# Another order for the first 200 steps of a fused window attention and gated MLP kernel on one core

## The chip, the cores and the metric

The kernel runs on one core of a Trainium2 chip. The core has five engines with their own instruction queues, each worked through in order: TensorE (PE in the profile; its weight loads are PEld), VectorE (DVE), ScalarE (ACT), GpSimd (POOL) and SyncE (SP). An engine waits on semaphores that other engines and the DMA transfers raise. SP and POOL issue all DMAs here. SP's go into one DMA queue (q1), POOL's into another (q0); POOL's are those that turn float32 in HBM into bfloat16 on the way.

The metric is the device time of one execution in microseconds, the median of several. The profile is of one execution.

## What is computed

Four batches, 8 heads, 768 positions, head size 64. Causal attention with a window of 128 and 4 sink positions, and behind it a block with a gelu, a layer norm over one half, a product over the positions (w_sg), a gate and an output product with a residual:

```python
scores = scale * np.matmul(q, k.transpose(0, 1, 3, 2))
keep = is_sink | in_window
scores = np.where(keep, scores, -1000000000.0)
a = softmax(scores)
x = heads_side_by_side(np.matmul(a, v))
...
h = gelu(x @ w_in)
u, v = (h[..., :d_ff // 2], h[..., d_ff // 2:])
v_n = (v - mu) / np.sqrt(var + 1e-06) * g_ln
v_s = np.einsum('ts,bsd->btd', w_sg, v_n) + b_sg[None, :, None]
return x + (u * v_s) @ w_out
```

## The kernel before

The kernel is one list of steps, `STEPS`, written out by hand. A step is a name and indices (`QK.0.1.2`: batch 0, head pair 1, group 2), and a last letter often gives the engine (A ScalarE, D VectorE, P GpSimd). A loop calls the function of each step in the order of the list; each engine then works through its own instructions in that order, with semaphores where data or buffers demand it. Nothing reorders them. So the list sets the order within each engine and within each DMA queue, and no more than that: a step of one engine may stand far ahead of another's and run later.

The stages of a batch, with the functions and their lines in the kernel before:

- **Loading q and k.** Batch 0 comes in as eight pairs of heads in float32 through SP (`LPQ`, `LPK`, L245, 384 KB each), is cast to bfloat16 by some engine (`CPQ`, `CPK`; `cast` and `copy`, L197 to L204), transposed on TensorE (`TQ`, `TK`, L376) and copied out of PSUM (`EQ`, `EK`, L199 and L200). Batches 1 to 3 come in as bfloat16 through POOL, in tiles of 128 positions with all heads (`LQ.b.i`, `LK.b.i`, L225, 128 KB written each). A transpose step of batch 1 or 2 (`TQ.b.g`, `TK.b.g`, L382) takes tiles 2g and 2g+1. Batch 3 is transposed by DMA (`DQ`, `DK`).
- **v and the weights.** `LVH.b.i` (L271) loads v of four heads through POOL, two per batch. `LW.0` and `LW.1` (L277) load the halves of w_in for v and for u, `LWS` (L282) the halves of w_sg, `LWO` (L285) w_out, `LB` (L301) b_sg. `LC` (L289) brings v's sink rows and `LG` (L292) the rows of g_ln through SP; `GTR` and `GCP` turn g_ln. POOL has eight semaphores for its loads, used in turn, so a load waits until the one eight before it has landed.
- **Attention.** `QK` (L483) makes the scores of two heads in one of two PSUM buffers (`sc`), `EX` (L488) the exponentials on ScalarE into one of ten `P` buffers. The window is cut out by `MK`: a product with a mask on VectorE (L495), or two selects on GpSimd (L498, L501). A `QK` step with a last index of 1 first multiplies the identity with a large negative bias (L478), and then needs no mask. `KS`, `SK` and `SX` do the sinks, `VSM` scales v's sink rows. `AV` (L524 to L531) multiplies with v into one of four PSUM buffers (`mm`), `NR` (L540, L541) divides by the sum. `XT` and `XE` transpose the result.
- **The block behind it.** `MV` and `GV` (L566, L570) make the v half of h and its gelu, `BN`, `RS`, `NM` and `Z` (L579 to L600) the layer norm, where `RS` runs on GpSimd. `MU` and `GU` (L607, L612) make the u half. `WT` and `WE` (L619) transpose w_sg. `SP` (L627) is the product over positions, `GT` and `GM` (L632, L637) the gate, `OU` (L644) the output product, `RA` the residual and `ST` the store.
- **Helpers.** `HM.n` puts n matmuls on zeros ahead of the next PSUM buffer's use (L190). `TBL` touches the exponential or gelu function, so that ScalarE loads its table there. `WARM`, `FILL`, `MASK`, `MASK0`, `VSK`, `VSO`, `ZERO`, `IDEN` and `IDEN2` set up constants.

The stages of neighbouring batches are interleaved: the steps of batch 0's gate run among batch 1's attention, and so on. Of batch 2's tiles, `LK.2.0` and `LK.2.1` feed `TK.2.0`, whose place on TensorE is between `SP.0.0.3` and `QK.1.2.1`.

The scores and the mask, as the code has them:

```python
def QK(b, p, g, biased=0):
    sc = fresh(sc_ring, (b, p, g))
    w = wide(g)
    if biased:
        for hl in range(2):
            nc.tensor.matmul(sc[:, hl, 0:w], iden, (bias1 if g else bias0)[:, 0:w], start=True, stop=False)
```

Of the kernel before, what the change touches and what calls it, by code (L numbers as in the profile page):

```python
# [25 lines left out]
MK.0.1.0.D SX.0.1 SX.0.2 QK.0.3.1 MK.0.2.1.P GCP.D NR.0.0.0 EX.0.3.0 AV.0.0.1 AV.0.1.0 AV.0.1.1 NR.0.0.1 EX.0.3.1
QK.0.1.2 NR.0.1.0 AV.0.2.0 AV.0.3.0 EX.0.1.2 MK.0.3.1.P NR.0.1.1 QK.0.2.2 AV.0.2.1 NR.0.2.0 EX.0.2.2 TQ.1.0 NR.0.3.0
MK.0.1.2.P QK.0.3.2 AV.0.3.1 EQ.1.0.A NR.0.2.1 XT.0.0 NR.0.3.1 LWS.0 AV.0.0.2 EX.0.3.2 TBL.G AV.0.1.2 XE.0.0.D LK.1.1
XT.0.1 MK.0.2.2.D MV.0.0 XE.0.1.A LK.1.2 NR.0.0.2 MK.0.3.2.D LK.1.3 NR.0.1.2 AV.0.2.2 AV.0.3.2 LQ.1.2 NR.0.2.2 GV.0.0
MV.0.1 NR.0.3.2 LQ.1.3 BN.0.0 LWS.1 XT.0.2 GV.0.1 MU.0.1 XE.0.2.A BN.0.1 WT.0 GU.0.1 TK.1.0 MV.0.2 RS.0.1 EK.1.0.A  # L30
LK.1.4 NM.0.1 WE.0.A WT.1 GV.0.2 LK.1.5 TK.1.1 MU.0.2 LB.P EK.1.1.A BN.0.2 Z.0.0.A LK.2.0 WT.2 GU.0.2 MU.0.0 WE.1.D
RS.0.2 WE.2.D Z.0.1.A LQ.2.0 NM.0.2 Z.0.2.A Z.0.3.D Z.0.4.D WT.3 LQ.2.1 WT.4 GU.0.0 TBL.E WE.3.D WT.5 LQ.1.4 Z.0.5.D
TQ.1.1 QK.1.0.0 EQ.1.1.D QK.1.1.0 LQ.1.5 SP.0.0.0 WE.4.D LK.2.1 EX.1.0.0 VSM.1 SP.0.0.1 WE.5.D EX.1.1.0 LVH.1.0
GT.0.0.0 TK.1.2 KS.1 GT.0.0.1 QK.1.2.0 QK.1.3.0 EX.1.2.0 SP.0.0.2 LVH.1.1 GM.0.0.0.D EX.1.3.0 MK.1.2.0.D TQ.2.0
EK.1.2.A LQ.2.2 QK.1.0.1 EQ.2.0.D QK.1.1.1 TQ.1.2 EX.1.0.1 GT.0.0.2 LWO SP.0.0.3 EQ.1.2.D EX.1.1.1 LK.2.2 MK.1.0.1.D
# [41 lines left out]
def kernel(  # L77
# [412 lines left out]
    def MK(b, p, g, e="D"):  # L490
        w = wide(g)
        pt = P[b, p, g]
        if e == "D":
# [7 lines left out]
        nc.gpsimd.affine_select(out=p4[:, :, :, 128:256], in_=p4[:, :, :, 128:256],  # L501
                                compare_op=ALU.is_ge, fill=0.0, base=-1,
                                pattern=[[0, 2], [0, 2], [-1, 128]], channel_multiplier=1)
# [212 lines left out]
```

## Time and profile before

| what | value |
|---|---|
| median of 3 runs | 155.82 us (155.35 to 155.89) |
| profiled execution | 155.89 us |
| its span in the trace | 154.2 us |
| instructions | 3867 |
| TensorE busy | 145.7 us (95%) |
| VectorE busy | 122.9 us (80%) |
| ScalarE busy | 100.0 us (65%) |
| GpSimd busy | 99.7 us (65%) |
| granted TensorE clock | 1.00 |
| POOL's DMA queue q0 | 11.01 MB in 64608 packets |
| SP's DMA queue q1 | 13.41 MB in 22552 packets |
| SP.0.0.0 starts (first L627) | 38.91 us |

Times in the profile are microseconds from the start of the span. A matmul's busy time includes the fill and drain of the array, and successive matmuls overlap, so a busy TensorE need not run at its peak rate. The views used below: the timeline of one engine (start, duration, engine and line, operation, tile written and tiles read, shapes, how many merged, and in brackets the idle time ahead of it with what ended it), the chain of waits (the work that ended last, followed back from the end), the waits by engine, and the DMA issues of a stretch of time with their time from issue to landing.

### The profile page before, as it was taken

What the parts mean: (1) busy time and instruction counts of PE and PEld (TensorE: products, weight loads), DVE (VectorE), ACT (ScalarE), POOL (GpSimd) and SP (SyncE); (2) the same over time, 40 slices, a digit from 0 to 9 for tenths busy, and PEclk for the clock granted to TensorE, in tenths of its full rate; (3) what the DMA queues carried; (4) which work ended last, traced back from release to release, by engine and by line L of the source; (5) the groups of instructions that cost most, each with busy time, mean ns of one, the idle gap of its engine ahead of it and who ended that gap; (6) DMA issues with size and microseconds to landing.
All of it is one profiled execution on the core that took longest, in us unless ns stands there. A gap on an engine that the chain in (4) does not pass through costs nothing.

```text
span 154.2 us, 3867 instructions
## 1 busy us (share of the span) xinstructions
PE 145.7 (95%) x1540; PEld 94.5 (61%) x1554; DVE 122.9 (80%) x296; ACT 100.0 (65%) x117; POOL 99.7 (65%) x127
## 2 busy tenths in 40 slices
PE   6899899999999988999899999999999999999990
PEld 2355586879675765758466764486567644775550
DVE  4666889739989977797799887899789957867992
ACT  3699998799899766456987865369957122491000
POOL 4099799298999699999469769640798610400400
PEclk9999999999999999999999999999999999999999
DMA  4999999999999999999999399996510582410055
GB/s 158 305 351 157 154 195 204 166 189 211 148 141 154 185 155 140 147 150 156 156 223 250 81 276 177 185 190 81 211 72 1 105 221 73 150 54 20 0 203 206
DMA packets 87178, 24.67 MB, mean 160 GB/s; under 512 B 78772, under 2 KB 84920, under 8 KB 87160
## 3 DMA queue, kind: packets, MB, share of 16 engines
q0 software_dynamic: 64608, 11.01, 95.7%
q1 hardware_dynamic: 22552, 13.41, 33.0%
q8 instruction: 12, 0.20, 0.5%
q14 instruction: 6, 0.05, 0.1%
HBM read 24.81 MB, written 6.29 MB: 202 GB/s over the span
## 4 chain that ended last, share of the span: by engine, by line
PE 54%; POOL 18%; DMA 15%; ACT 4%; DVE 4%; issue 2%; SPq 1%; DVEq 0%; ACTq 0%; POOLq 0%
PE mm L627 15%; DMA v_sb<-in_v_dram 11%; PE mm L644 10%; PE sc L566 9%; PE sc L607 8%; POOL q L225 5%; POOL k L225 4%; DMA uT<-in_k_dram 4%; PE sc L483 4%; PE mm L524 3%; POOL v_sb L271 3%; PE mm L528 2%; POOL wsg_gated L637 2%; POOL P L498 2%; POOL P L501 2%
## 5 line engine op out<-in xcount | busy, mean ns | idle before, releaser
L488 ACT ACTIVATE P<-sc 128x1024 bf16<-128x1024 f32 (+1 forms) x48 | 43.4, 952 | 10.3 <-PE sc L483 10.1
L627 PE MATMUL mm<-wsgT,z 128*128 128x384 bf16 x192 | 34.4, 327 | 0.3 <-ACT z L597 0.3
L627 PEld LDWEIGHTS <-z 128*128 128x128 bf16 x192 | 17.6, 98 | 12.5 <-issue 0.7
L570 ACT ACTIVATE vt<-sc 128x1024 f32<-128x1024 f32 x12 | 12.3, 1027 | 18.4 <-PE sc L566 18.4
L632 DVE SCALAR_TENSOR_TENSOR gtmp<-mm,g_sb,b_bc 128x384 bf16<-128x384 f32 x32 | 19.0, 610 | 4.2 <-PE mm L627 4.0
L637 POOL TENSOR_TENSOR wsg_gated<-gtmp,uT 128x384 bf16<-128x384 bf16 x15 | 14.9, 1006 | 11.3 <-DVE gtmp L632 11.2
L607 PE MATMUL sc<-xT,w_in_sb 128*128 128x256 bf16 x192 | 22.1, 273 | 0.0
L566 PE MATMUL sc<-w_in_sb,xT 128*128 128x512 bf16 x92 | 21.8, 379 | 0.2
L644 PE MATMUL mm<-w_out_sb,wsg_gated 128*128 128x512 bf16 x85 | 21.2, 379 | 0.5
L498 POOL TENSOR_SCALAR_AFFINE_SELECT P<-P 128x512 bf16<-128x512 bf16 x21 | 13.7, 653 | 11.4 <-ACT P L488 11.4
L607 PEld LDWEIGHTS <-w_in_sb 128*128 128x128 bf16 x192 | 18.7, 98 | 2.9
L579 DVE BATCH_NORM_STATS2 st<-vt 128x6 f32<-128x512 f32 x24 | 15.4, 685 | 6.1 <-ACT vt L570 6.0
L541 DVE TENSOR_TENSOR x_sb<-mm,rcp 128x384 bf16<-128x384 f32 (+1 forms) x36 | 18.5, 513 | 1.2
L588 POOL TENSOR_TENSOR rs<-rs,neg_half 128x4 f32<-128x4 f32 (+1 forms) x8 | 7.1, 882 | 15.8 <-DVE rs L583 14.4
L225 POOL DMA_DIRECT2D k<-in_k_dram x18 | 16.4, 924 | 1.3 <-DMA v_sb<-in_v_dram 1.3
L648 DVE TENSOR_TENSOR ot<-mm,x_sb 128x512 f32<-128x512 f32 x23 | 15.4, 683 | 2.2 <-PE mm L644 2.2
L225 POOL DMA_DIRECT2D q<-in_q_dram x18 | 16.8, 956 | 0.0
L524 PE MATMUL mm<-v_sb,P 128*128 128x65 bf16 x192 | 16.1, 194 | 0.6 <-DVE x_sb L541 0.4
L524 PEld LDWEIGHTS <-P 128*128 128x128 bf16 x192 | 14.5, 97 | 2.5 <-DMA v_sb<-in_v_dram 0.6
L528 PE MATMUL mm<-v_sb,P 128*128 128x65 bf16 x160 | 15.4, 193 | 0.4 <-POOL P L501 0.4
L612 ACT ACTIVATE uT<-sc 128x1024 bf16<-128x1024 f32 x12 | 12.2, 1024 | 5.1 <-PE sc L607 5.1
L566 PEld LDWEIGHTS <-xT 128*128 128x128 bf16 x96 | 9.2, 98 | 10.1
(92 smaller groups left out, 242.9 us busy)
## 6 DMA issues: line engine op xcount, KB each, us to landing
out_dram<-ot SPq DMA_DIRECT2D x17, 256.0 KB, 2.5
v_sb<-in_v_dram POOLq DMA_DIRECT2D x8, 384.0 KB, 8.0
q<-in_q_dram POOLq DMA_DIRECT2D x18, 128.0 KB, 6.5
k<-in_k_dram POOLq DMA_DIRECT2D x18, 128.0 KB, 7.3
out_dram<-ot SPq DMA_DIRECT2D x14, 128.0 KB, 1.8
wsg_gated<-in_moe_w_sg_dram POOLq DMA_DIRECT2D x2, 576.0 KB, 8.4
w_in_sb<-in_moe_w_in_dram POOLq DMA_DIRECT2D x2, 512.0 KB, 9.0
uT<-in_q_dram SPq DMA_DIRECT2D x2, 384.0 KB, 3.0
```

The lines of the kernel that those rows point to most:

```text
L225: return nc.gpsimd.dma_start(out=dst.rearrange("p (h d) -> p h d", h=H), in_=heads(src, b, i))
L488: nc.scalar.activation(out=P.new((b, p, g))[:, :, 0:w], in_=sc_ring[b, p, g][:, :, 0:w], func=AF.Exp, scale=scale)
L498: nc.gpsimd.affine_select(out=p4[:, :, :, 0:128], in_=p4[:, :, :, 0:128], compare_op=ALU.is_ge, fill=0.0, base=0, pattern=[[0, 2], [0, 2], ...
L524: nc.tensor.matmul(av[:, il, hl, :], pt[:, hl, c:c + 128], vb[:, h, i, :], start=first, stop=False)
L528: nc.tensor.matmul(av[:, il, hl, :], pt[:, hl, c:c + 128], vb[:, h, i - 1, :], start=False, stop=(i < 2 and il == n - 1 and hl == 1))
L541: nc.vector.tensor_mul(x_sb.get(b)[:, i0:i0 + n, 128 * p:128 * (p + 1)].rearrange("p t (h d) -> p t h d", h=2), av[:, :, :, 0:Dh], rcp[:, ...
L566: nc.tensor.matmul(hp[:, jl, :], xT[b][:, 2 * g + jl, c, :], w_in_sb[:, c, d_half:2 * d_half], start=(c == 0), stop=(c == KD - 1))
L607: nc.tensor.matmul(hp[:, dc // 2, 256 * (dc % 2):256 * (dc % 2 + 1)], w_in_sb[:, c, 128 * dc:128 * (dc + 1)], xT[b][:, 2 * g:2 * g + 2, c, :],
L627: nc.tensor.matmul(ps[:, 0:NH], z[b][:, si, 128 * dc:128 * (dc + 1)], wsgT[:, si, NH * hf:NH * (hf + 1)], start=(si == 0), stop=(si == NT ...
L632: nc.vector.scalar_tensor_tensor(out=gtmp.new((b, hf, dc)), in0=mm_ring["g", b, hf, dc][:, 0:NH], scalar=g_sb[:, dc:dc + 1], in1=b_bc[:, N ...
L637: (nc.vector if e == "D" else nc.gpsimd).tensor_mul(gated(b, hf)[:, dc, :], gtmp[b, hf, dc], uT[b][:, dc, NH * hf:NH * (hf + 1)])
L644: nc.tensor.matmul(ps, gated(b, hf)[:, dc, 128 * tl:128 * (tl + 1)], w_out_sb[:, dc, :], start=(dc == 0), stop=(dc == KU - 1))
```

## The change

The first 200 or so steps are the same work in another order, up to `QK.1.3.0 EX.1.2.0`; from `SP.0.0.2` on the list is the same. The last letters and some forms differ:

- SP's loads are K0 Q0 G Q1 Q2 K1 K2 K3 Q3 (pairs of q and k, and `LG`) in place of Q0 K0 K1 Q1 Q2 G K2 K3 Q3.
- The casts of k pairs 0 and 1 and 2 are on VectorE (before: ScalarE, GpSimd, ScalarE), that of q pair 1 is on GpSimd (before: VectorE). GpSimd's `LVH.0.0` and `LVH.0.1` follow the cast of q pair 1 in place of that of k pair 1.
- `EQ.0.0` and `EQ.0.1` are on ScalarE, `EQ.0.2` on VectorE; before it was the other way round. `XE.0.0` is on ScalarE, `XE.0.1` and `XE.0.2` on VectorE.
- `QK.0.0.0` and `QK.0.1.0` are made with the bias, `QK.0.1.1` without it. The step `MK` with the letter N does nothing and marks such a group. `MK.0.1.1` and `MK.0.2.2` are on GpSimd; `MK.0.2.1` and `MK.0.1.2` on VectorE.
- `HM` counts are 9, 1, 1, 1, 2, 1, 2, 1 in place of 9, 4, 1, 3, 1, 3. Four of the new ones stand behind `AV.0.0.0`.
- The two `SK` steps stand behind `AV.0.1.0`, before they stood ahead of `AV.0.0.0`.
- `TQ.1.1` stands where `TQ.1.0` stood, and `TQ.1.0` later.
- The gelu table is loaded directly ahead of `GV.0.0`, the exponential's directly ahead of `EX.1.1.0`.
- POOL's loads behind `LVH.0.1`, as its queue has them:

```
before  LQ.1.0 LQ.1.1 LW.0 LK.1.0 LW.1 LWS.0 LK.1.1 LK.1.2 LK.1.3 LQ.1.2 LQ.1.3 LWS.1 LK.1.4 LK.1.5 LB LK.2.0 LQ.2.0 LQ.2.1 LQ.1.4 LQ.1.5 LK.2.1 LVH.1.0 LVH.1.1 LQ.2.2 LWO
after   LQ.1.3 LQ.1.2 LW.0 LWS.0 LW.1 LQ.1.1 LK.1.2 LQ.1.0 LK.1.1 LK.1.0 LWS.1 LQ.2.0 LK.1.4 LK.1.3 LK.1.5 LB LQ.1.4 LQ.2.1 LQ.1.5 LVH.1.0 LK.2.0 LK.2.1 LVH.1.1 LQ.2.2 LWO
```

- `RS.0.1` stands on GpSimd behind `LB` and ahead of `LQ.1.4`, `RS.0.2` between `LQ.1.5` and `LVH.1.0`; before, `RS.0.1` stood ahead of `LK.1.4` and `RS.0.2` ahead of `LQ.2.0`.

The diff, with the step list cut to the lines that are new:

```diff
-WARM LPQ.0 FILL LPK.0 LPK.1 LPQ.1 LPQ.2 LG MASK LPK.2 LPK.3 CPQ.0.A VSK LPQ.3 IDEN CPK.0.A IDEN2 MASK0 HM.9 TQ.0.0
-TK.0.0 EQ.0.0.D EK.0.0.A VSO HM.4 QK.0.0.0 ZERO CPK.1.P QK.0.0.1.1 EX.0.0.0 LVH.0.0 EX.0.0.1 QK.0.0.2.1 CPQ.1.D TK.0.1
...
+WARM LPK.0 LPQ.0 LG LPQ.1 CPQ.0.A IDEN FILL LPQ.2 CPK.0.D IDEN2 MASK ZERO HM.9 TK.0.0 EK.0.0.A HM.1 TQ.0.0 MASK0 VSK
+GTR VSO EQ.0.0.A HM.1 QK.0.0.0.1 EX.0.0.0 QK.0.0.1.1 CPQ.1.P LPK.1 TQ.0.1 QK.0.0.2.1 MK.0.0.0.N CPQ.2.D LPK.2 GCP.D
+EQ.0.1.A CPK.1.D EX.0.0.1 TK.0.1 LVH.0.0 TQ.0.2 CPK.2.D EQ.0.2.D LPK.3 LVH.0.1 TK.0.2 EK.0.1.A QK.0.1.0.1 CPK.3.P
+LQ.1.3 EX.0.0.2 LPQ.3 QK.0.1.1 EX.0.1.0 EX.0.1.1 LQ.1.2 TK.0.3 CPQ.3.D EK.0.2.D EK.0.3.A LW.0 TQ.0.3 HM.1 QK.0.2.1
+EX.0.2.1 QK.0.2.0 HM.2 AV.0.0.0 LC MK.0.0.1.N MK.0.1.0.N VSM.0 HM.1 AV.0.1.0 EQ.0.3.D KS.0 EX.0.2.0 SK.0.1 QK.0.3.1
+NR.0.0.0 SX.0.1 SK.0.2 NR.0.1.0 EX.0.3.1 MK.0.1.1.P AV.0.0.1 MK.0.2.0.D QK.0.3.0.1 AV.0.2.0 LWS.0 MK.0.2.1.D QK.0.1.2
+LW.1 SX.0.2 LQ.1.1 AV.0.1.1 NR.0.0.1 EX.0.3.0 NR.0.2.0 QK.0.2.2 MK.0.3.0.N AV.0.3.0 AV.0.2.1 MK.0.0.2.N EX.0.1.2
+MK.0.3.1.P NR.0.1.1 AV.0.3.1 QK.0.3.2 NR.0.3.0 NR.0.2.1 XT.0.0 LK.1.2 EX.0.2.2 XE.0.0.A NR.0.3.1 MK.0.2.2.P HM.2
+TQ.1.1 LQ.1.0 LK.1.1 XT.0.1 LK.1.0 AV.0.2.2 EX.0.3.2 LWS.1 AV.0.0.2 EQ.1.1.A MV.0.0 VSM.1 MK.0.1.2.D LQ.2.0 AV.0.1.2
+LK.1.4 XE.0.1.D MK.0.3.2.D GV.0.0 NR.0.0.2 NR.0.2.2 AV.0.3.2 LK.1.3 LK.1.5 NR.0.3.2 MV.0.1 NR.0.1.2 TBL.G.1 GV.0.1
+BN.0.0 XT.0.2 LB.P XE.0.2.D WT.1 BN.0.1 MU.0.1 MV.0.2 RS.0.1 WE.1.A WT.2 LQ.1.4 NM.0.1 TK.1.0 GU.0.1 MU.0.2 GV.0.2
+WE.2.D BN.0.2 HM.1 TQ.1.0 WT.3 Z.0.3.A MU.0.0 EK.1.0.A KS.1 LQ.2.1 Z.0.0.A EQ.1.0.D LQ.1.5 RS.0.2 GU.0.2 WT.0 LVH.1.0
+WT.4 TK.1.1 Z.0.2.A NM.0.2 Z.0.1.D Z.0.4.D LK.2.0 WE.3.A WE.0.D WT.5 WE.4.D Z.0.5.D GU.0.0 QK.1.1.0 LK.2.1 QK.1.0.0
+SP.0.0.1 WE.5.D EK.1.1.D SP.0.0.0 EX.1.1.0 TK.1.2 GT.0.0.1 QK.1.2.0 TBL.E.1 GT.0.0.0 EX.1.0.0 QK.1.3.0 EX.1.2.0
 SP.0.0.2 LVH.1.1 GM.0.0.0.D EX.1.3.0 MK.1.2.0.D TQ.2.0
...
-    def TBL(func):
+    def TBL(func, turn):
...
     def MK(b, p, g, e="D"):
         w = wide(g)
         pt = P[b, p, g]
+        if e == "N":
+            return
...
-        ps = mm_ring["o", b, t] if h else fresh(mm_ring, ("o", b, t))
+        ps = mm_ring["o", b, t] if ("o", b, t) in mm_ring.held else fresh(mm_ring, ("o", b, t))
```

More of the change, by code (lines that the diff above doesn't have):

```diff
@@ L26 @@
[L26 to L35, printed above, removed]
@@ new lines @@
+WT.4 TK.1.1 Z.0.2.A NM.0.2 Z.0.1.D Z.0.4.D LK.2.0 WE.3.A WE.0.D WT.5 WE.4.D Z.0.5.D GU.0.0 QK.1.1.0 LK.2.1 QK.1.0.0
+SP.0.0.1 WE.5.D EK.1.1.D SP.0.0.0 EX.1.1.0 TK.1.2 GT.0.0.1 QK.1.2.0 TBL.E.1 GT.0.0.0 EX.1.0.0 QK.1.3.0 EX.1.2.0
+SP.0.0.2 LVH.1.1 GM.0.0.0.D EX.1.3.0 MK.1.2.0.D TQ.2.0 EK.1.2.A LQ.2.2 QK.1.0.1 EQ.2.0.D QK.1.1.1 TQ.1.2 EX.1.0.1
+GT.0.0.2 LWO SP.0.0.3 EQ.1.2.D EX.1.1.1 LK.2.2 MK.1.0.1.D TK.2.0 MK.1.0.0.D QK.1.2.1 LK.2.3 EK.2.0.A QK.1.3.1
+MK.1.3.0.D SK.1.0 GM.0.0.1.D LQ.2.3 SP.0.1.0 EX.1.2.1 GT.0.0.3 MK.1.1.0.D LQ.2.4 EX.1.3.1 SP.0.1.1 MK.1.1.1.D LQ.2.5
@@ new lines @@
+MK.2.3.0.D TQ.2.1 LVH.2.0 TQ.2.2 EQ.2.1.D MV.1.0 EQ.2.2.D LQ.3.0 EK.2.2.D LQ.3.1 VSM.2 MU.1.0 GV.1.0 MK.2.1.0.D
+LVH.2.1 BN.1.0 MV.1.1 GU.1.0 LQ.3.2 RA.0.2 LQ.3.3 MK.2.0.0.D MV.1.2 GV.1.1 MK.2.2.0.D LK.3.1 KS.2 LK.3.2 BN.1.1 MU.1.1
+GV.1.2 LK.3.3 BN.1.2 RS.1.1 MU.1.2 GU.1.1 LQ.3.4 NM.1.1 Z.1.0.A RS.1.2 OU.0.3 GU.1.2 TBL.E.2 LQ.3.5 NM.1.2 Z.1.1.D
+SK.2.0 Z.1.4.D QK.2.0.1 Z.1.2.D Z.1.3.A QK.2.1.1 Z.1.5.D OU.0.4 RA.0.3 DK.3.0 SP.1.0.0 RA.0.4 SX.2.0 EX.2.0.1 SP.1.0.1
+GT.1.0.0 DQ.3.0 EX.2.1.1 GM.1.0.0.D SP.1.1.0 MK.2.0.1.P GT.1.0.1 QK.2.2.1 ST.0.3 GT.1.1.0 QK.2.3.1 GM.1.0.1.P DQ.3.1
```

63 lines of the change are left out of this document (27 added, 36 removed).

## The prediction

> **What bounds the kernel now.** I read, in order: the chain of waits (what the end hangs on), the timeline of each engine, and the DMA issues of short windows (issue to landing of one transfer). The profiled execution took 155.89 us: span 154.2 and 1.7 around it; the median of the runs is 155.82, so 0.07 less.
>
> The chain, us from start, length, what:
>
> ```profile
> 1.81 5.80 DMA uT<-in_k_dram
> ...
> 7.69 0.79 POOL k L204
> 8.48 8.04 DMA v_sb<-in_v_dram
> ...
> 42.11 9.21 DMA v_sb<-in_v_dram
> 51.36 0.50 issue
> 51.85 1.82 POOL k L225 x2
> ...
> 71.34 1.06 POOL rs L588
> ```
>
> Up to 16.5 us the end hangs on a load: the third pair lands at 7.61, POOL casts it, and only then issues v (LVH), which lands 8 us later. The chain comes back to POOL's loads from 36 to 52 us.
>
> TensorE, where it had to wait (timeline: start, us, operation, idle before and who ended it):
>
> ```profile
> 45.36 0.61 PE L382 MATMUL mm<-iden,k 128*128 128x128 bf16 x8
> ...
> 54.20 1.04 PE L644 MATMUL mm<-w_out_sb,wsg_gated 128*128 128x512 bf16 x3
> ...
> 55.83 0.40 PE L382 MATMUL mm<-iden,k 128*128 128x128 bf16 x4 [0.37 <-DMA k<-in_k_dram]
> ...
> 58.51 0.20 PE L528 MATMUL mm<-v_sb,P 128*128 128x65 bf16 x1 [0.39 <-POOL P L501]
> ```
>
> The first of these lines is step TK.2.0. Otherwise TensorE is full: busy 23.38 us of 16 to 40, 73.19 of 77 to 154. So a step's shift reaches the end unless one of these waits takes it up.
>
> Issues of a short window (KB, us from issue to landing):
>
> ```profile
> v_sb<-in_v_dram POOLq DMA_DIRECT2D x1, 384.0 KB, 7.2
> k<-in_k_dram POOLq DMA_DIRECT2D x1, 128.0 KB, 4.8
> ```
>
> These are LVH.1.0 and LK.2.1, and POOL issued them so:
>
> ```profile
> 39.85 0.91 POOL L225 DMA_DIRECT2D k<-in_k_dram  x1
> 40.71 2.86 POOL L271 DMA_DIRECT2D v_sb<-in_v_dram  x2
> ```
>
> So LK.2.1 landed at 39.85 + 4.8 = 44.6, LVH.1.0 at 40.71 + 7.2 = 47.9, LVH.1.1 at 42.11 + 9.2 = 51.3. Read one by one, POOL's loads land strictly in their order of issue, without a break, from LVH.0.0 (16.5) to LWO (54.2): a k or q tile lands 0.85 us after the one before it, a half of v 2.9 to 3.4, a half of w_in 2.5 to 2.6, of w_sg 2.8. This queue is full; a load's landing is its place in it.
>
> **The change part by part.**
>
> *Start of the queue.* LPQ.1 takes LPK.1's place as third pair, with the 2 KB of LG before it. Pairs landed at 3.85, 5.0, 7.6, 8.7, 9.7 (ends of the waits of their casts), two issues ahead of the data, so I take LG at nothing: third pair 7.6, POOL cast 0.8, LVH issued at 8.5, v at 16.5, all as before. GTR now needs g_rows before QK.0.0.0, at 6.4. Its landing there isn't shown: between 5.0 (pair ahead) and 7.6 (pair behind), 0 to 1.2; I take 0, and up to 16.5 the wait for v covers it.
>
> *ScalarE and VectorE until v.* ScalarE loses the casts of k pairs 0 and 2 (2 x 0.83) and gains EQ.0.0 and EQ.0.1, losing EQ.0.2 (+0.8): 0.86 less. VectorE gains three k casts (0.56 each), loses a q cast, the copies of EQ.0.0 and EQ.0.1 (0.95 each) and one 0.54 mask, and gains EQ.0.2. Followed pair by pair, k pair 1 is now fifth (9.7) and EK.0.1 ends near 11.5, against 11.3 before; EX.0.2.0 and .1, the seventh and eighth exponentials, end near 16.8, against 16.9. Nothing on the path. One more biased product of 384 columns (two matmuls, 0.33) lies there too.
>
> *TensorE after v.* The first AV starts at 16.56 as before. Behind it now stand HM.1, HM.2 and HM.1 (4 warm matmuls; a warm 128x512 starts every 0.216 us: 0.86) and the two SK groups that ran at 16.03 while TensorE waited (0.40): 1.26 more. Before had one wait in this part, 0.39 at 19.44, that these fill in part. The gelu table load (1.28) moves to directly ahead of GV.0.0, where MV.0.0 (1.7) runs over it; without that cover it would cost 1.28. WT, MU and MV change places among themselves; each load they need is due 0.5 us or more before it is used (LWS.0 and LW.1 follow LW.0, which landed at 22.9: 22.9 + 2.8 + 2.5 = 28.2, used at 29.3; LK.1.0 is five tiles later, 28.2 + 5 x 0.85 = 32.4, used at 33.3). So SP.0.0.1 starts 0.8 to 1.3 later; I take 1.1, near 40.0.
>
> *Loads of POOL.* This decides. Before, the end of this stretch was LK.2.0, LQ.2.0, LQ.2.1, LQ.1.4, LQ.1.5, LK.2.1, LVH.1.0, LVH.1.1. Now it is LVH.1.0, LK.2.0, LK.2.1, LVH.1.1. Ahead of LVH.1.1 stand the same 24 loads in both kernels; the 24th was LVH.1.0 and is now LK.2.1. It inherits that landing: 47.9 in place of 44.6. POOL's own waits don't break the queue: a load waits for the landing of the one eight before it, so LVH.1.0 is issued at about 37 and LK.2.1 by 40.2, in time; RS.0.1, behind LB, waits until 31.6 (before: 30.67), which the shift above holds.
>
> TK.2.0 reads LK.2.1. TensorE came to it at 45.36, now at 46.5 with the 1.1; it must stand until 47.95. All behind it (QK.1.2.1, QK.1.3.1, SK.1.0, SP.0.1.0) is late by 47.95 - 45.36 = 2.6, and the 1.1 is inside that. On ScalarE EK.2.0 and EX.1.2.1 wait with it, on VectorE MK.1.2.1.
>
> *What takes it up.* OU.0.0 waited for w_out until 54.2, TK.2.1 for k until 55.83, AV.1.3.1 for a POOL mask until 58.51. Places and landings of these loads are unchanged, POOL's masks too (its chain starts at 51.85, after LVH.1.1). Idle time there is 0.16 (the QK ahead ends at 54.04) + 0.37 + 0.39 = 0.92; start to start against the usual step it is 0.2 + 0.5 + 0.5 = 1.2, which I take. Left: 1.4. At 76.67 SP waits for z:
>
> ```profile
> 76.67 1.64 PE L627 MATMUL mm<-wsgT,z 128*128 128x384 bf16 x9 [0.26 <-ACT z L597]
> ```
>
> That z stood behind RS.1.1, which POOL began at 71.3 though its input was ready at 70.6; 1.4 later it begins at 72.0, so 0.35 more is taken up. Left 1.05. Behind that the order is unchanged and TensorE full, so it reaches the end.
>
> Sum: 155.89 + 2.6 - 1.2 - 0.35 = 156.94; beside the median, **156.9 us**.
>
> A clock row: the first nine warm matmuls ran in 3.71 us (0.42 each), later ones start every 0.216, and the granted clock is 1.00 in every window. The change has 14 warm matmuls ahead of the first AV where 21 stood (9 of them at the start in both); between 9.8 and 11.7 TensorE has only transposes.
>
> By the Trainium skill (TensorE: Matmul & The Clock Gate, Parts 1 and 4) an idle window of about 3.4 us brings the half clock back, and transposes don't count as busy in the same way; this gap would be under 2.5 us, so by that rule the sum stays.
>
> **The rivals.**
>
> - *Nothing takes up the 2.6.* VectorE is 4.00 busy of 4.00 at 44 to 48 and 48 to 52; held back by MK.1.2.1 it might be the next bound. Against: it waits 0.73 at 56.8 for TensorE, and most of its work there doesn't hang on TK.2.0. 155.9 + 2.6 = 158.5.
> - *Not slower: the queue starts earlier.* The third pair took 2.6 us behind the second, all others 1.0 to 1.2. If that was k's own bad luck, q pair 1 lands at 6.2; POOL's queue and all landings come 1.4 earlier. LK.2.1 lands at 46.5, TK.2.0 is 1.2 late, the three waits take that up, and a little of the wait for z too: 155.5. It decides from a landing of q pair 1 below 6.5 (1.05 gained); with 2 us gained (v at 14.5) it would be 154.9. For it: the odd 2.6. Against: it may belong to the third place.
> - *The queue doesn't pass the delay on* (LK.2.1 by 46.5, though behind LVH.1.0). Then 1.1 is left, which the 1.2 takes up: 155.8. Against: every landing read is in order.
> - *The half clock returns* for some 3.4 us ahead of the first AV: 1.7 of TensorE's time there, of which the wait for v hides half. TensorE would still be early enough for TK.2.0 at 47.95, so little is added: 157.3.
>
> **How the numbers follow.** Forecast 0.47; nothing taken up 0.14; earlier queue 0.25 (0.15 of it below 155.04); order not passed on 0.09; clock 0.05. The forecast's own range is 156.4 to 157.5 (uptake 0.9 to 1.3 and 0 to 0.4, landing +-0.4). Both signs hold chance, so the range goes from 155.0 (most of the earlier queue) to 158.6 (nothing taken up). About 0.5%, 0.78 us, is what a measurement can tell from no change: above 156.60 lie nearly four fifths of the forecast, the second and the last rival, 0.55; below 155.04 0.15; between 0.30.
>
> **What would show it.** Right: LVH.0.0 issued near 8.5 and the first AV near 16.5; LK.2.1 landing near 47.9; TensorE idle 1 to 2 us ahead of TK.2.0 with k's load as releaser; no wait left at 54.2, 55.8 and 58.5; z's wait near 77.7. Wrong: TK.2.0 without a wait, LVH.0.0 issued before 7.5, or SP.0.0.1 over 2 us later than 38.9.

## The result and the profile after

The changed kernel took 157.19 us (median of 4 runs, 157.07 to 157.55), the kernel before 155.58 us beside it (154.69 to 155.89): ratio 1.0117, 95% interval 1.0069 to 1.0164. A repeat of 12 runs on another occasion gave 1.0076 (1.0052 to 1.0101). So the change costs about 1%, 1.2 to 1.8 us. All ratios leave out runs more than 1.5% above the fastest of the same kernel. The profiled execution took 157.07 us, span 155.4, granted clock 1.00. The forecast of 156.9 us was near. Its mechanism was not the one that ran.

The chain of waits of the changed kernel (us from start, length, what), the answer to the first lines shown of before:

```profile
2.25 4.40 DMA uT<-in_q_dram
6.74 0.83 POOL q L205
7.57 1.84 POOL v_sb L272
9.41 9.13 DMA v_sb<-in_v_dram
...
46.55 2.25 DVE P L498 x3
48.80 0.98 DVE wsg_gated L640
49.79 0.54 DVE gtmp L635
50.37 1.14 PE mm L630 x6
```

The third pair, now q, landed at 6.65 (2.25 + 4.40), not at 7.6, so v was issued at 7.57 and not at 8.48. POOL's loads have left the chain around 42 to 52 us; three groups of VectorE (DVE) stand there instead.

TensorE of the changed kernel (timeline: start, us, operation, idle before and what ended it):

```profile
40.98 1.31 PE L630 MATMUL mm<-wsgT,z 128*128 128x384 bf16 x7 [0.34 <-DVE z L603]
...
46.61 0.61 PE L383 MATMUL mm<-iden,k 128*128 128x128 bf16 x8
...
50.37 0.81 PE L630 MATMUL mm<-wsgT,z 128*128 128x384 bf16 x4 [1.18 <-DVE gtmp L635]
...
56.58 1.04 PE L647 MATMUL mm<-w_out_sb,wsg_gated 128*128 128x512 bf16 x3
57.45 0.61 PE L383 MATMUL mm<-iden,k 128*128 128x128 bf16 x8
...
77.93 0.82 PE L630 MATMUL mm<-wsgT,z 128*128 128x384 bf16 x4 [0.37 <-ACT z L600]
```

TK.2.0 (46.61) has no bracket: it waited for nothing. LK.2.1 had landed at 46.4, read from its semaphore. The long wait is at 50.37, SP.0.1.1, which needs a PSUM buffer that GT.0.0.3 empties on VectorE. From 56 to 58 us the waits of before are gone: TensorE is later, and w_out and k were there earlier (w_out at 52.30 for 54.15 before, the later k tile of TK.2.1 at 53.97 for 55.78).

VectorE just ahead of that (same columns), in the changed kernel:

```profile
45.35 0.61 DVE L635 SCALAR_TENSOR_TENSOR gtmp<-mm,g_sb,b_bc 128x384 bf16<-128x384 f32 x1
45.87 0.68 DVE L201 COPY qT<-mm 128x1024 bf16<-128x1024 bf16 x1
46.47 2.33 DVE L498 TENSOR_TENSOR P<-P,mask 128x1024 bf16<-128x1024 bf16 x3
48.73 1.06 DVE L640 TENSOR_TENSOR wsg_gated<-gtmp,uT 128x384 bf16<-128x384 bf16 x1
49.71 0.60 DVE L635 SCALAR_TENSOR_TENSOR gtmp<-mm,g_sb,b_bc 128x384 bf16<-128x384 f32 x1
```

and POOL beside it:

```profile
45.81 2.64 POOL L226 DMA_DIRECT2D q<-in_q_dram  x3 [0.34 <-DMA v_sb<-in_v_dram]
48.44 1.13 POOL L640 TENSOR_TENSOR wsg_gated<-gtmp,uT 128x384 bf16<-128x384 bf16 x1
```

In the kernel before, POOL reached the same product a microsecond later:

```profile
46.88 2.72 POOL L225 DMA_DIRECT2D q<-in_q_dram  x3
49.50 1.03 POOL L637 TENSOR_TENSOR wsg_gated<-gtmp,uT 128x384 bf16<-128x384 bf16 x1
```

VectorE's lines are GT.0.0.2, EQ.1.2, three masks, GM.0.0.1, GT.0.0.3. The three masks took 2.33 us and GM.0.0.1 1.06; in the kernel before the same took 1.62 and 0.35:

```profile
44.09 0.61 DVE L632 SCALAR_TENSOR_TENSOR gtmp<-mm,g_sb,b_bc 128x384 bf16<-128x384 f32 x1
...
45.22 1.62 DVE L495 TENSOR_TENSOR P<-P,mask 128x1024 bf16<-128x1024 bf16 x3
46.75 0.35 DVE L637 TENSOR_TENSOR wsg_gated<-gtmp,uT 128x384 bf16<-128x384 bf16 x1
47.02 0.61 DVE L632 SCALAR_TENSOR_TENSOR gtmp<-mm,g_sb,b_bc 128x384 bf16<-128x384 f32 x1
```

From GT.0.0.2 to GT.0.0.3 it is 2.93 us before and 4.36 after. GM.0.0.1 began inside POOL's GM.0.0.2 (48.44 to 49.57) and ended 0.22 after it. Before, POOL's GM.0.0.2 ran at 49.50, 2.5 us behind GT.0.0.3. POOL is now 1.1 us earlier and VectorE 1.26 us later (TensorE is): they meet. POOL isn't earlier because its queue began earlier: its RS.0.2 ran at 36.49, before at 35.40, and in the profile of a_heat, with a first AV at 16.98, GM.0.0.2 still ran at 48.45. The records show that in the changed order POOL issues 11 loads between RS.0.2 and GM.0.0.2, and before 14. The other 0.71 us is a mask, MK.1.0.0, that took 1.26 in place of 0.55 and by the records ended at 48.33, just ahead of POOL's product; what held it up isn't clear (last section).

So the difference of the two spans, stage by stage (start times of steps, us):

| kernel | first AV | to first SP | to SP.0.1.0 | to SP.0.1.1 | to end | span |
|---|---|---|---|---|---|---|
| before | 16.56 | 22.35 | 7.87 | 0.99 | 106.39 | 154.16 |
| changed | 15.55 | 24.11 | 8.37 | 2.34 | 105.00 | 155.37 |
| difference | -1.01 | +1.76 | +0.50 | +1.35 | -1.39 | +1.21 |

Of the +1.76, 0.34 us is a wait of TensorE at 18.58 for the second half of v. In the +0.50 stands the wait for z at 40.98 (0.34 idle). The chain behind it goes back through VectorE's copies of z (the one at 37.79 took 1.36 us where 0.54 is usual) and POOL's RS.0.2 to a load that POOL held back until LWS.1 had landed at 35.31.

### The profile page after: what moved, and what is told of

Same layout as the page of the kernel before. It is cut to its first block, busy times and chain, and to the rows that moved or that the text cites. A ratio compares the mean times of both kernels' runs of the same rounds, so it can differ in the third digit from the quotient of the medians.

```text
span 155.4 us, 3858 instructions
## 1 busy us (share of the span) xinstructions
PE 146.4 (94%) x1539; PEld 94.9 (61%) x1553; DVE 127.1 (82%) x297; ACT 98.1 (63%) x115; POOL 99.7 (64%) x127
## 4 chain that ended last, share of the span: by engine, by line
PE 60%; DMA 15%; DVE 10%; POOL 5%; ACT 4%; issue 2%; SPq 1%; DVEq 0%; ACTq 0%
PE mm L630 18%; PE mm L647 12%; PE sc L569 9%; PE sc L610 8%; DMA wsg_gated<-in_moe_w_sg_dram 7%; DMA v_sb<-in_v_dram 6%; PE sc L484 5%; PE mm L527 3%; DMA uT<-in_q_dram 3%; DVE P L498 2%; PE mm L531 2%; PE mm L383 2%; DVE z L603 2%; DVE st L582 2%; PE mm L534 1%
## 5 line engine op out<-in xcount | busy, mean ns | idle before, releaser
L484 PE MATMUL sc<-qT,kT 64*128 64x128 bf16 (+1 forms) x256 | 15.0, 238 | 0.8 <-ACT P L489 0.5
```

The source lines that it names most:

```text
L484: nc.tensor.matmul(sc[:, hl, c:c + 128 * ni], at(kT, b)[rows, j, p, :], at(qT, b)[rows, i:i + ni, p, :], start=not biased, stop=(not biase ...
```

## The experiments

The theories: A, TensorE stands for VectorE's late GT.0.0.3 (A2: which is late because of POOL's product beside it); C, the load order, as predicted; G, the extra TensorE work behind the first AV. Ratios are to the kernel before, run beside each. The stages of each profile, as in the table above:

| run | ratio (95%) | first AV | to first SP | to SP.0.1.0 | to SP.0.1.1 | to end |
|---|---|---|---|---|---|---|
| a_gt | 1.0048 (1.0015 to 1.0081) | 16.04 | 23.98 | 7.87 | 0.99 | 105.70 |
| a_loads | 1.0082 (1.0054 to 1.0111) | 17.01 | 23.81 | 7.87 | 0.98 | 105.52 |
| b_loads | 1.0121 (1.0067 to 1.0175) | 16.40 | 22.13 | 11.13 | 1.60 | 105.02 |
| b_third | 1.0012 (0.9983 to 1.0041) | 17.35 | 22.99 | 7.87 | 0.99 | 105.63 |
| a_same | 1.0076 (1.0052 to 1.0101) | 15.88 | 23.89 | 8.32 | 2.05 | 105.01 |
| b_work | 1.0050 (1.0022 to 1.0077) | 16.82 | 23.20 | 7.86 | 0.99 | 106.02 |
| a_heat | 1.0084 (1.0054 to 1.0115) | 16.98 | 23.18 | 8.19 | 2.33 | 105.04 |
| a_gm | 1.0042 (1.0012 to 1.0071) | 17.50 | 23.86 | 7.87 | 0.98 | 105.01 |
| b_lg | 0.9961 (0.9932 to 0.9990) | 16.07 | 22.28 | 7.87 | 0.98 | 105.73 |
| a_gmheat | 1.0675 (1.0623 to 1.0726) | 17.02 | 23.19 | 8.18 | 0.99 | 116.49 |

**a_loads: the load order undone.**

```diff
-LQ.1.5 RS.0.2 GU.0.2 WT.0 LVH.1.0 ... LK.2.0 ... LK.2.1
+LQ.1.5 RS.0.2 GU.0.2 WT.0 LK.2.0 LK.2.1 LVH.1.0
```

> The changed kernel with the load order of before in this one place: LK.2.0 and LK.2.1 are issued ahead of LVH.1.0 again. Theory C (the predicted one: the place of LK.2.1 behind half a v tile sets the time of TK.2.0 and with it the loss): LK.2.1 lands about 3 us earlier, near 43.4, and the kernel comes back to 155.6 to 156.2. Theory A (VectorE's lateness at GT.0.0.3 sets it; TK.2.0 ran at 46.61 without a wait, LK.2.1 having landed at 46.4): the loads land earlier, TensorE's order of waits is the same, 157.2 within 0.4.

The time did not come back: 1.0082, beside 1.0117 and 1.0076 of the changed kernel. So the place of LK.2.0 and LK.2.1 isn't what costs the time in the changed kernel (C). In its profile the wait at SP.0.1.1 is gone, since POOL, which now issued other loads first, ran GM.0.0.2 only at 49.41, behind GT.0.0.3 (48.92). That profile had a first AV at 17.01, 1.1 to 1.5 us later than the two of the changed kernel, and so the same span. Why the other nine runs show no gain either isn't settled. It speaks against the wait at SP.0.1.1 as the main loss: here the wait is gone and the time is not.

**b_loads: the load order alone, on the kernel before.**

```diff
-LK.2.0 ... LQ.1.5 ... LK.2.1 ... LVH.1.0 GT.0.0.0
+LQ.1.5 ... LVH.1.0 LK.2.0 LK.2.1 GT.0.0.0
```

> The kernel before with the load order of the change in that one place: LK.2.0 and LK.2.1 are issued behind LVH.1.0. Theory C (the mechanism as predicted, on the queue of before, which starts with v at 8.5): LK.2.1 lands near 47.9 in place of 44.6, TensorE stands about 2.4 us ahead of TK.2.0, which ran at 45.36, the waits near 54.2, 55.8 and 58.5 take up about 1.2 of it, and the time is 156.4 to 157.0. Rival (loads don't inherit the place: k lands by 46.5): 155.6 within 0.4. It also tells whether the predicted step was wrong in itself, or right and absent only because the queue of the changed kernel starts earlier.

TensorE in this kernel, and its granted clock (windows: busy us and instruction counts of PE, PEld, DVE, ACT, POOL, then PEclk, DMA share, GB/s):

```profile
46.72 0.40 PE L382 MATMUL mm<-iden,k 128*128 128x128 bf16 x4 [1.58 <-DVE wsg_gated L637]
47.61 0.61 PE L382 MATMUL mm<-iden,k 128*128 128x128 bf16 x4 [0.49 <-DMA k<-in_k_dram]
```

```profile
46.00:48.00 2.00, 0.79 (x8) 0.57 (x8) 2.00 (x5) 0.00 (x0) 2.00 (x3) 0.88 2.45 156
48.00:50.00 2.00, 2.00 (x21) 0.93 (x19) 0.31 (x1) 1.75 (x2) 2.00 (x4) 0.50 2.37 162
```

The predicted mechanism is real in before's order of the other loads: LK.2.0 landed at 46.7, LK.2.1 at 47.6 (predicted 47.9), and TensorE stood at TK.2.0 for both. (The first bracket names a VectorE step that ended long before; k is what came last.) It cost more than predicted: 1.0121, and that without the three longest of its six runs. The extra cost goes with the clock. Of the six, the one with a granted clock of 1.00 took 156.92 us, inside the 156.4 to 157.0 of the expectation; the other five took 157.98 to 160.53 us at 0.98 to 0.99. In the profile the granted clock was 0.88 from 46 to 48 us and 0.50 from 48 to 50. If it was full until it fell to the half, it fell near 47.5 (an estimate from the 0.88). By the Trainium skill (TensorE: Matmul & The Clock Gate, Part 1) about 3.4 us of idle bring the half clock; here it came some 2.4 us after the last matmul other than transposes (45.1), with idle pieces of 1.58 and 0.49 and four transposes between them.

**a_gt: VectorE's GT.0.0.3 three steps earlier.**

```diff
-TK.2.0 MK.1.0.0.D ... MK.1.3.0.D ... GM.0.0.1.D ... EX.1.2.1 GT.0.0.3 MK.1.1.0.D
+TK.2.0 GT.0.0.3 MK.1.0.0.D ... MK.1.3.0.D ... GM.0.0.1.D ... EX.1.2.1 MK.1.1.0.D
```

> The changed kernel with one VectorE step moved: the copy GT.0.0.3 stands directly ahead of the mask MK.1.0.0 in place of behind MK.1.0.0, MK.1.3.0 and GM.0.0.1. Theory A (what costs the time now is VectorE: TensorE stood 1.18 us at 50.37 because GT.0.0.3, which frees the buffer of SP.0.1.1, ran at 49.71): GT.0.0.3 runs near 47.1, SP.0.1.1 starts near 49.2 without a wait, and the kernel comes back by 0.8 to 1.2 us, to 156.0 to 156.4. Rival B (VectorE is full, 4.00 busy of 4.00 in 44 to 48 and 48 to 52, so a step moved ahead only moves the wait to the next step that needs VectorE): a wait of about 1 us appears at GT.0.1.0, GM or the masks of batch 1, and the time stays 157.2 within 0.3. Rival C (the order of POOL's loads, as predicted): no effect, 157.2.

GT.0.0.3 ran at 46.93, SP.0.1.1 had no wait, and the ratio fell to 1.0048. A mask still met POOL's product (1.26 us in place of 0.55, at 48.12), but nothing on TensorE waited for it. Theory A holds in direction. The gain, against 1.0076 and 1.0117, is 0.3 to 0.7% (0.4 to 1.1 us), where 0.8 to 1.2 us was expected, and the interval overlaps that of the repeat, so this run alone doesn't prove it.

**a_gm: POOL's product GM.0.0.2 later.**

```diff
-EX.1.0.2 GM.0.0.2.P SP.0.1.2 GT.0.1.1 EX.1.1.2 LK.2.4 GM.0.1.0.D
+EX.1.0.2 SP.0.1.2 GT.0.1.1 EX.1.1.2 LK.2.4 GM.0.0.2.P GM.0.1.0.D
```

> The changed kernel with one POOL step moved: the product GM.0.0.2 runs on POOL behind the load LK.2.4 in place of ahead of it, near 51 us in place of 48.2. VectorE's order and TensorE's are untouched. Theory A2 (what makes GT.0.0.3 late is VectorE's GM.0.0.1 and a mask running at half speed or less beside POOL's product: 1.06 and 1.27 us in place of 0.36 and 0.55): GM.0.0.1 takes 0.36 us, GT.0.0.3 starts 0.7 or more earlier against GT.0.0.2 (3.6 or less in place of 4.36 us), and the wait at SP.0.1.1 falls from 1.06 to 1.39 to under 0.6; the time falls by up to 0.7 us, less what the product stretches near 51 us. Rival I (the stretch has nothing to do with POOL's product): GM.0.0.1 stays near 1.06 us and the wait at 1.1 to 1.4.

VectorE in this kernel:

```profile
46.54 0.61 DVE L635 SCALAR_TENSOR_TENSOR gtmp<-mm,g_sb,b_bc 128x384 bf16<-128x384 f32 x1
47.06 0.68 DVE L201 COPY qT<-mm 128x1024 bf16<-128x1024 bf16 x1
47.66 1.62 DVE L498 TENSOR_TENSOR P<-P,mask 128x1024 bf16<-128x1024 bf16 x3
49.20 0.35 DVE L640 TENSOR_TENSOR wsg_gated<-gtmp,uT 128x384 bf16<-128x384 bf16 x1
49.47 0.61 DVE L635 SCALAR_TENSOR_TENSOR gtmp<-mm,g_sb,b_bc 128x384 bf16<-128x384 f32 x1
```

With POOL's product away, the masks take 1.62 us again and GM.0.0.1 0.35, with VectorE's own order untouched; GT.0.0.3 is 2.93 us behind GT.0.0.2 as before, and SP.0.1.1 waits for nothing. So POOL's product beside it made VectorE slow (A2), GM.0.0.1 plainly; the mask is slow with the product there and not without it, but how the product reached it isn't shown. The profiled execution had a first AV at 17.50 and so a span like the changed kernel's (155.2); the gain is read from the ratio alone. The ratio 1.0042 is of eight of twelve runs (155.87 to 157.09 us); the other four took 165.84 to 168.00 us, for a cause that the run a_gmheat suggests.

**a_same: the changed kernel once more.**

> The changed kernel as it is, once more, for a second profile and times beside the others. If the early third load (6.65) belongs to the changed order: third pair by 6.8 and first AV near 15.5 again, with waits at z (40.98) and at SP.0.1.1 (50.37) of 0.3 and 1.2 us. If it was chance (other profiles of the same order show it at 6.9 and 7.7, those of before's order at 7.4, 7.6 and 8.6): another landing, the first AV moves with it by as much, and the waits at z and SP.0.1.1 shrink by what the first AV is later, the time staying near 157.2.

Third pair at 7.1, first AV at 15.88, again a wait at SP.0.1.1 (0.90 idle) with the same 4.36 us from GT.0.0.2 to GT.0.0.3. Here the predicted wait shows in small: LK.2.1 landed at 46.84, and TensorE, which began TK.2.0 at 46.38, stood about 0.28 us inside it.

**b_work: the extra TensorE work alone, on the kernel before.**

```diff
-HM.3 SK.0.2 EX.0.2.1 SK.0.1 MK.0.2.0.D AV.0.0.0
+EX.0.2.1 MK.0.2.0.D HM.3 AV.0.0.0 SK.0.2 SK.0.1
...
-AV.0.1.0 ... TQ.1.0 ... TK.1.0
+HM.1 AV.0.1.0 ... HM.2 TQ.1.0 ... HM.1 TK.1.0
```

> The kernel before with the predicted extra work alone: the sink groups SK.0.2 and SK.0.1 directly behind AV.0.0.0 in place of ahead of it, and warm matmuls HM.1 ahead of AV.0.1.0, HM.2 ahead of TQ.1.0 and HM.1 ahead of TK.1.0 (1.26 us in all). Nothing of loads, casts or masks is changed. The prediction's sum with the load step taken out: the first SP is 1.1 late, the waits near 54, 56 and 58 us take up all of it, and the ratio to before is 1.000 within 0.003. Theory G (in most executions the slack there is already used up by a late start of the queue): ratio 1.005 to 1.009. Theory A (VectorE alone costs it, which the 1.1 makes late): a wait of over 0.5 us at SP.0.1.1 in the trace, and ratio over 1.005.

Ratio 1.0050: 0.8 us, where the prediction's sum would give nothing. VectorE shows no wait at SP.0.1.1, so this is not A. In its profile the first SP came 0.85 later behind the first AV, and what lies behind SP.0.1.1 took up only 0.37 of it, in place of 1.39 in the changed kernel. The work costs by itself, as G says. The waits near 56 and 59 us stay in part (0.16 and 0.39 idle), because the loads that end them came 0.6 to 0.8 us later too: POOL's RS.0.2 ran at 36.47 for 35.40, and w_out landed at 54.78 for 54.15, TK.2.1's k at 55.80 for 54.96, LVH.1.1 at 52.08 for 51.32. So part of TensorE's lateness comes back through POOL's queue.

**a_heat: the four warm matmuls behind the first AV taken away.**

```diff
-HM.1 AV.0.1.0 ... HM.2 TQ.1.1 ... HM.1 TQ.1.0
+AV.0.1.0 ... TQ.1.1 ... TQ.1.0
```

> The changed kernel without the three sets of warm matmuls behind the first AV (HM.1 ahead of AV.0.1.0, HM.2 ahead of TQ.1.1, HM.1 ahead of TQ.1.0: 4 matmuls, 0.86 us of the predicted 1.26); the sink groups stay behind the first AV. Theory G (TensorE's extra work behind v is the loss): AV to the first SP falls from 23.9 to 24.1 us in two profiles by 0.8 to 0.9, and the ratio falls from 1.008 to 1.012 by 0.005, to 1.003 to 1.006. Theory A2 (VectorE and GpSimd meet: POOL runs GM.0.0.2 beside VectorE's GM.0.0.1 because POOL is early and VectorE late, which stretches it by 0.7 us): VectorE comes 0.8 earlier and misses POOL's GM.0.0.2, so the wait at SP.0.1.1 (1.1 to 1.4) shrinks to under 0.3 as well, ratio 0.997 to 1.002. Rival H (loads hold the place): TK.2.0 waits 0.5 to 0.8 for k and nothing is gained.

From the first AV to the first SP 0.7 to 0.9 us were gained, and no time: 1.0084. The wait at SP.0.1.1 stayed (1.18 idle). In this profile a late first AV (16.98) had eaten the 0.8, so VectorE came to POOL's product as late as in the changed kernel and met it with the mask MK.1.3.0 instead of GM.0.0.1; both stand ahead of GT.0.0.3. The A2 part of the expectation (a miss of POOL's product) fell, and G with it as a gain that can simply be taken out. SP.0.1.1 started at 50.37, 50.14 and 50.68 in the three profiles with this meeting, though their first AVs lay at 15.55, 15.88 and 16.98: POOL's product, at 48.44, 48.19 and 48.45, seems to set it, not the first AV. (In a_work, with the same meeting, SP.0.1.1 came at 52.49 and the product at 49.74, so the distance is 1.9 to 2.8 us and not one number.)

**a_gmheat: both edits.**

> The changed kernel with both edits: GM.0.0.2 behind LK.2.4 on POOL, and the four warm matmuls behind the first AV gone. It asks whether those 0.86 us of TensorE count once VectorE and GpSimd no longer meet ahead of GT.0.0.3; alone their removal gave nothing (1.0084 beside 1.0076 and 1.0117), the wait at SP.0.1.1 stayed at 1.35. Theory K (that wait swallowed them: TensorE came 0.8 earlier and stood for the late GT.0.0.3 all the same): no wait over 0.4 us at SP.0.1.1, AV to the first SP near 23.1 us, ratio 0.998 to 1.001, 0.5 to 0.9 us below the run with GM.0.0.2 moved alone (1.0042). Rival L (the warm matmuls cost nothing, since loads or VectorE set the time from 24 us on): ratio 1.003 to 1.005 again, with TensorE waiting at TK.2.0 or for z instead.

It took 7% longer. VectorE, POOL and the windows of this kernel:

```profile
52.33 0.68 DVE L498 TENSOR_TENSOR P<-P,mask 128x1024 bf16<-128x1024 bf16 x1
52.93 5.12 DVE L640 TENSOR_TENSOR wsg_gated<-gtmp,uT 128x384 bf16<-128x384 bf16 x1
57.98 0.61 DVE L635 SCALAR_TENSOR_TENSOR gtmp<-mm,g_sb,b_bc 128x384 bf16<-128x384 f32 x1
```

```profile
53.06 0.66 POOL L501 TENSOR_SCALAR_AFFINE_SELECT P<-P 128x512 bf16<-128x512 bf16 x1
...
57.21 0.63 POOL L504 TENSOR_SCALAR_AFFINE_SELECT P<-P 128x512 bf16<-128x512 bf16 x1
```

```profile
56.00:60.00 4.00, 1.36 (x22) 1.25 (x21) 3.93 (x7) 0.00 (x0) 3.17 (x6) 0.74 0.85 52
60.00:64.00 4.00, 3.78 (x31) 2.46 (x31) 2.50 (x6) 1.20 (x2) 3.88 (x5) 0.50 0.72 74
```

GM.0.0.3, a product of 0.35 us, came to VectorE as POOL began eight selects in a row, and ended 0.21 after the last of them (57.84): 5.12 us. TensorE stood 4.14 us for the GT behind it, and half the clock followed (PEclk 0.74, then 0.50); a second stand, 2.88 us, came at 77. In the profile of a_gm the same GM.0.0.3 ran at 53.59 in 0.35 us, and POOL's selects began at 53.73. The product's record starts ahead of the first select in both, by 0.13 and by 0.14 us, so the start alone doesn't decide. What differs in the records is that POOL stood idle for 0.14 us ahead of its first select in a_gm and went into it straight from a load's issue in a_gmheat; whether that decides isn't shown. The four long runs of a_gm had the same lowered clock (0.97 to 0.98) and the same spans (164 to 166); that they met in this way is an inference. Up to SP.0.1.1 the profile goes as theory K says (no wait there, first AV to first SP 23.19 us), but the total can't tell K from L, and whether the warm matmuls would cost their 0.86 us there stays open.

**b_third and b_lg: the first loads, on the kernel before.**

```diff
-b_third: LPK.0 LPK.1 LPQ.1 LPQ.2 ... CPK.1.P ... CPQ.1.D
+b_third: LPK.0 LPQ.1 LPK.1 LPQ.2 ... CPQ.1.P ... CPK.1.D
...
-b_lg: LPK.0 LPK.1 LPQ.1 LPQ.2 LG MASK
+b_lg: LPK.0 LG LPK.1 LPQ.1 LPQ.2 MASK
```

> The kernel before with q pair 1 as third load and k pair 1 as fourth (their casts change places too: POOL casts q pair 1, VectorE k pair 1), and nothing else. In the profile of before the third pair landed at 7.6 and v was issued at 8.48; in the changed one it landed at 6.65 and v was issued at 7.57. Theory D (it is the order of the two first pairs and the k pair that makes the third late, and an earlier third load brings the whole queue forward): third pair by 6.7, first AV near 15.6, time 154.6 to 155.2. Rival E (the third place itself, or chance, is late): third pair near 7.6, first AV near 16.5, time 155.6 within 0.4. Rival F (it lands earlier, but what stands behind the first AV takes the 1.0 back): first AV near 15.6 and time 155.6.

With q as third pair it landed at 8.6, later than any other, and the ratio is 1.0012: q or k makes no difference (D is out).

> The kernel before with the small load LG ahead of the third pair in place of behind the fifth, and nothing else. Seven profiles with that place (all of the changed order) had the third pair at 6.5, 6.5, 6.65, 6.9, 7.1, 7.7 us and the like; four with before's place had it at 7.4, 7.6, 7.6 and 8.6, whether the third was k or q. Theory J (the place of LG sets it): third pair by 7.1, first AV by 16.1, and as the waits for loads near 54 and 56 us move with the queue the time falls by 0.4 to 0.8 us, ratio 0.995 to 0.998. Rival E (chance from execution to execution, or another of the first loads): third pair near 7.6 and ratio 1.000 within 0.003.

(The profiles of the changed order at hand then were six: 6.5, 6.5, 6.65, 6.9, 7.1 and 7.7.) The chain of b_lg begins:

```profile
2.26 4.71 DMA uT<-in_k_dram
7.05 0.83 POOL k L204
7.88 1.76 POOL v_sb L271
```

Third pair at 6.97, v issued at 7.88, and a ratio of 0.9961 (0.9932 to 0.9990): 155.43 us beside 155.76. It is the one version that beat both kernels. An earlier v, as theory J has it, is seen in its one profile (first AV 16.07), which is one of its fastest runs (154.63 us). But further profiles of the changed order had the third pair at 7.6, 7.7 and 8.0, so the place of LG doesn't fix the landing, and how it shifts the odds is open.

**a_work and a_best: the sink groups ahead of the first AV again.** In both the PSUM buffers go round once more before SX.0.2 reads, so that its exponentials are those of other numbers; the amount of work is the same.

```diff
-QK.0.2.0 HM.2 AV.0.0.0 ... HM.1 AV.0.1.0 EQ.0.3.D KS.0 EX.0.2.0 SK.0.1 QK.0.3.1 NR.0.0.0 SX.0.1 SK.0.2
+QK.0.2.0 KS.0 EQ.0.3.D SK.0.1 SK.0.2 HM.2 AV.0.0.0 ... AV.0.1.0 EX.0.2.0 QK.0.3.1 NR.0.0.0 SX.0.1
```

> The changed kernel with the predicted extra TensorE work taken away from behind the first AV: no warm matmuls HM.1, HM.2, HM.1 there (4 matmuls, 0.86 us), and the two sink groups SK.0.1 and SK.0.2 (with KS.0 and EQ.0.3 that they need) ahead of AV.0.0.0 as in the kernel before (0.40 us). Theory G (the loss is this work: from the first AV to MV.0.0 the changed kernel took 8.1 to 8.3 us in three profiles, before took 6.7 to 7.5, and the three waits near 54 to 58 us hide little of it in most executions): AV to MV.0.0 near 7.1, and the ratio to before falls from 1.012 to 1.002 or below, about 1.3 us faster than the changed kernel. Theory A (the wait at SP.0.1.1 for VectorE, wherever its lateness comes from): TensorE comes to SP.0.1.1 earlier and VectorE too, since it follows TensorE, so part is gained, 0.3 to 0.8 us. Rival H (a wait for z at 40.98 and the loads hold the place): TensorE waits longer for z or k and nothing is gained.

> The changed kernel with three mendings together: the extra work behind the first AV taken away (as in the run above), GT.0.0.3 ahead of MK.1.0.0, and POOL's RS.0.2 ahead of the load LQ.1.5, which made it wait for a landing until 35.3. If the three causes add (1.2 for the work, 0.8 for GT.0.0.3, 0.3 for the wait for z, together more than the loss): ratio to before 0.990 to 0.998, since the first AV no longer depends on anything else and only the waits for loads near 54 and 56 us can hold it. If they are one cause seen at three places (TensorE late from 16 to 24 us): the same as the run above, within 0.3 us.

Both failed as experiments: TensorE now stood idle ahead of the sink groups, 1.13 and 0.97 us for VectorE's KS.0 and 0.58 us for its EQ.0.3, the first AV slid to 17.9, and the ratios were 1.0158 and 1.0098. In the changed order the sink groups can't stand ahead of the first AV, since their inputs aren't ready. The wait at SP.0.1.1 was there in a_work (1.39 us start to start over the usual step) and gone in a_best, which has GT.0.0.3 moved. That RS.0.2 ahead of LQ.1.5 is worth something alone was not tried.

## Why the prediction was right in its number and wrong in its way

- *Start of the queue.* Predicted: third pair 7.6, v issued 8.5, first AV 16.5, "all as before". Measured: 6.65, 7.57, 15.55. Its fault is to read one landing as a fixed price. Left to itself the first AV began between 15.55 and 17.50 in seven profiles of the changed order, and between 16.40 and 17.35 in four of before's.
- *TensorE after v.* The 1.26 us of extra work were named rightly, the step was mis-sized: 1.1 more up to the first SP was taken, and it was 1.5 to 1.8 (23.89 and 24.11 beside 22.35). In the first profile 0.34 of it is a wait for the second half of v that the sum doesn't have. The warm matmuls hold 0.7 to 0.9 of it (a_heat).
- *Loads of POOL ("This decides").* This is the step that failed: LK.2.1 was to inherit its place's landing of 47.9, and TensorE to stand at TK.2.0 until then. Alone on the kernel before it holds almost to the number (b_loads: landing 47.6, a stand at TK.2.0). In the changed order LK.2.1 landed at 46.41, behind LVH.1.0 at 45.52 and LK.2.0 at 45.86, and TensorE came to its half of TK.2.0 only at about 46.8: no wait, the prediction's own sign of being wrong.

  An earlier start of the queue doesn't explain it. In six profiles of the changed order LK.2.1 landed between 46.2 and 47.3, at 46.7 and 46.8 also where v began to land 0.4 us later than before's 16.52 (a_heat and a_gmheat), and 47.3 where it was 0.9 later (a_gm). Nor do loads follow each other "without a break" by the price of the load: in before's own profile LQ.1.4 landed 1.60 us behind LQ.2.1, and LQ.2.2 only 0.26 behind LVH.1.1; here LK.2.0 and LK.2.1 came 0.34 and 0.55 behind the load ahead, not 0.85. So a place in the queue did not fix the landing once the loads ahead of it were in another order; what sets it there is open. The places and landings of the later loads weren't unchanged either (LVH.1.1 at 49.49 for 51.32). Undoing the order gave nothing back (a_loads).

  The rival of the earlier queue asked for a landing below 6.5; it was 6.65, and the 1.0 us gained there was spent behind it. The rival "the queue doesn't pass the delay on" asked for LK.2.1 by 46.5 and had it; its 155.8 us missed, since it has neither VectorE's lateness at GT.0.0.3 nor the whole of the work after v.
- *What took its place.* SP.0.1.1 was 2.6 us late (47.77 to 50.37), as TK.2.0 was to be, by chance: 1.25 from TensorE's own lateness, with the wait for z at 40.98 in it that the sum left out, and 1.35 from VectorE, held up while POOL ran GM.0.0.2 close by. The prediction saw VectorE busy for 4.00 of 4.00 us and counted it only as a bound if all lateness were kept; it did not ask what POOL would do beside it once both had shifted. Moving either of the two colliding steps (a_gt, a_gm) brings the ratio from between 1.008 and 1.012 down to between 1.004 and 1.005.
- *What takes it up.* The three waits near 54, 56 and 58 us: 1.2 predicted, 1.39 measured. This was right in size. But the loads that end these waits moved as well, 1.8 us earlier here and 0.6 to 0.8 later in b_work, where only 0.37 of 0.85 was taken up.
- *The wait for z at 76.67.* Predicted to give 0.35; measured none (idle 0.26 before, 0.37 after).
- *Clock.* As forecast, 1.00 throughout. It fell in b_loads and a_gmheat, behind stands of TensorE that the changed kernel doesn't have.

The sum as predicted was 2.6 - 1.2 - 0.35 = 1.05. The sum as it ran is -1.01 + 1.76 + 0.50 + 1.35 - 1.39 = 1.21. That VectorE comes late to GT.0.0.3 beside POOL's product, and that TensorE stands for it, is shown by the traces and by a_gm. What it is worth, about half of the loss, is an estimate: a_gt and a_gm point the same way, their intervals touch the repeat's, and a_loads lost the wait and gained nothing. The extra work behind the first AV costs 0.5% alone on the kernel before. That the two add up to the loss isn't shown, since a_heat gained nothing.

## What to carry to other kernels

When a change shifts two engines in opposite directions, lay their timelines over each other and look for pairs of operations that will newly run side by side, above all VectorE products with both inputs in SBUF beside GpSimd's work. A landing early in a kernel is a spread, not a number: take it from several profiles before a later step is made to hang on 0.2 us. A load's place in a queue gives its landing only as long as the loads ahead of it stay as they were. And a mechanism shown alone (b_loads) doesn't prove that it acts in the whole change.

## What was not expected of the hardware

Where a VectorE product with both inputs in SBUF met POOL's work here, it did not end before it: it ended 0.21 to 0.23 us after POOL's instruction (GM.0.0.1 in the changed kernel, GM.0.1.0 in the kernel before at 50.27, where 0.35 became 0.49), a mask about 0.4 after it. The Trainium skill (SBUF — State Buffer, Who interferes with whom) says that a VectorE instruction with two SBUF inputs and a GpSimd instruction that reads SBUF exclude each other, and that the one that comes second is blocked. For GM.0.0.1 of the changed kernel, which began 0.29 us behind POOL's product, the trace agrees. In a_gmheat it is less plain, since VectorE's record starts 0.13 us ahead of POOL's first select, and the loss went beyond one instruction: VectorE got no turn between eight instructions of POOL, 5.12 us in place of 0.35.

One thing fits this less well. In the changed kernel the mask MK.1.0.0 also took 1.26 us in place of 0.55 (47.07 to 48.33) while the records show POOL only issuing loads (in a_same and a_heat its end reached 0.4 and 0.2 us into POOL's product); with POOL's product moved (a_gm) it took 0.55 beside the same kind of issues. And VectorE's z copy at 37.79 took 1.36 us in place of 0.54 beside POOL's issue of half a v tile (37.18 to 38.93), in most profiles of the changed load order, and 0.8 us where another load's issue stood there (a_loads, a_best); no experiment took that apart.

The landing of the third pair varied from 6.5 to 8.6 us over the fourteen profiles. In the late ones, read from when the parts of each load landed, one to three of the 16 DMA engines ran up to 2 us behind the others from an early pair on and stayed behind through the pairs that followed (in the kernel before, 13 parts of the third pair were there by 6.6 and the last at 7.6).
